# Attention operands laid out by the host: transposes on the chip, a buffer of parts and two early weight conversions taken out of a fused attention, MoE and mixer kernel

## The chip, the cores and the metric

The kernel runs on one core of a Trainium2 chip. The metric is device time in microseconds of one execution, the median of the runs. The engines are TensorE (PE in the profile; its weight loads are PEld), VectorE (DVE), ScalarE (ACT), GpSimd (POOL) and SyncE (SP, which here only issues DMAs). Each engine runs its own instructions strictly in order.

## The reference

Four batches of 576 positions, 8 heads of 64, model width 512. Cut to what is computed:

```python
# attention: q, k, v (4, 8, 576, 64), s (4, 8, 576)
scores = q @ k.T / sqrt(64)
cum = cumsum(maximum(s, 0))                       # along the sequence
scores = where(causal, -1e9, scores + minimum(-(cum_i - cum_j), 0))
attn = softmax(scores);  x = attn @ v             # heads side by side: (4, 576, 512)
# MoE: 8 experts, w1 (8, 512, 1024), w2 (8, 1024, 512); each position goes to one expert e,
# its own argmax or that of the position before, by a gate
x = p[e] * (maximum(x @ w1[e], 0) @ w2[e])
# mixer: U (576, 32), V (32, 576), w_ch1 (512, 2048), w_ch2 (2048, 512)
u = x + (x^T @ U @ V)^T
out = u + maximum(u @ w_ch1, 0) @ w_ch2
```

The inputs come in fp32; w_ch1 and w_ch2 are float64 in memory and come as 8-byte words.

## The kernel before

**Precision by parts.** Each fp32 operand of a large product is split into a high part (a rounded copy, made by ACT, tile type fp32r or f16) and a low part (the operand less its high part, made by DVE or POOL). A product is then high x high + high x low + low x high.

**Stages in time.** Attention with the router runs from 0 to about 290 us, the routing tail (positions scattered to the rows of their experts in DRAM) from there to 323, expert 0 to 367, the other experts to 590, the mixer to the end.

**Attention.** The 32 heads are taken as 16 pairs of neighbouring heads. For a pair n, an operand tile `OP[n % NB]`, with NB = 2, holds four blocks of 576 columns for each head: K1, Q1, K2, Q2, where rows 0 to 63 and 64 to 127 hold different parts, so that one matmul over 128 rows (L706) takes two of the three partial products of the scores and a second over 68 rows (L713) takes the third with the cumulative bias in four more rows. The bias rows come from DRAM (`b_d`, read by `bias(n)` L443). The scores need the head dimension on the partitions, while q and k lie in memory with the position on the rows. So `prep(n)` (L448) does, for each pair:

- loads of two pairs at a time (a group of four heads) into kn, qn, vn, tiles of 128 positions x 5 blocks x 4 heads x 64, in runs of 256 bytes (`load_group` L377, DMAs at L361);
- ten transposes on PE (`blocks`, L468) into PSUM tiles `pt`;
- four ACT copies out of PSUM, the high parts, into a tile `parts` of four blocks, 448 and 128 columns wide (`high`, L475);
- four DVE instructions, the low parts (`low`, L480);
- four DMAs on SP that copy the parts into the operand tile, each head's parts to both halves of the partitions where needed (`stack`, L538, 2 x 576 + 2 x 288 KB). Pair 2 uses free weight tiles (`ring`) in place of `parts`, and twelve DMAs. One `parts` tile exists, so ACT's high parts of the next pair wait until these DMAs have read it (`hold`).

Pair 0 has a path of its own (L1284 to L1325): ACT and DVE copy each head twice side by side, PE transposes the doubled tile, and ACT, DVE and POOL split straight into OP.

The softmax runs in units of one tile of 128 queries and one or two heads: scores on PE into `sp`, the row extremum `nm` on DVE (L730), the exponential on ACT into `Pb` (L747), transposes of it on PE into `pp` (L776), their high part on ACT (`hi`, L784) and low part on DVE (`lo`, L789), the product with V on PE into `ob` (L825), its copy by ACT into `xr` (L837). V is scaled and split on POOL into `VP` (L620 scale, L630 high, L640 low).

**What sets the order.** All of this is recorded as some 1,680 jobs and issued by a table of job numbers, ORDER (L29 to L124), which fixes what stands before what on every engine. The jobs are checked for buffers: `issue` allows a job only when the one that frees its place stands earlier.

**Weights.** Expert weights come in units of 128 columns of w1 (`load_in` L205, DMA L207, 512-byte runs) or 128 rows of w2 (`load_out` L213, DMA L216) into five `raw` buffers, and `conv` (L222) splits a unit into a `ring` tile, high at L226 (POOL) or L230 (ACT), low at L233 (DVE or POOL). Eight units of w1 of expert 0 and, with NEARLY = 2, two units of w2 are converted by POOL beside the attention. The other six units of w2 are converted at the end of the routing tail: four by ACT and DVE, and two by POOL (at 328 to 333 us).

## Time and profile before

| | us |
|---|---|
| three runs | 1011.66, 1013.52, 1017.26 |
| median | 1013.52 |
| the profiled execution itself | 1015.48 |
| its span in the trace | 1013.5 |

| busy in the span | PE | DVE | ACT | POOL |
|---|---|---|---|---|
| us | 936.4 | 567.8 | 453.6 | 361.6 |
| share | 92% | 56% | 45% | 36% |

The page gives one execution. Its shares are means over stages that differ much: DVE and ACT are half busy over the whole, but three quarters busy in the attention and a third or less in the mixer. So the windows by stage are read before any share. A wait is listed with what ended it; an engine that waits costs time only where PE, or whatever stands last in that stage, waits for it in turn. A row of a timeline gives the start, the length, the engine, line, instruction, the tile written and the tile read, and in brackets the idle time just before with its releaser.

### The profile page before, as it was taken

What the parts mean: (1) busy time and instruction counts of PE and PEld (TensorE: products, weight loads), DVE (VectorE), ACT (ScalarE), POOL (GpSimd) and SP (SyncE); (2) the same over time, 40 slices, a digit from 0 to 9 for tenths busy, and PEclk for the clock granted to TensorE, in tenths of its full rate; (3) what the DMA queues carried; (4) which work ended last, traced back from release to release, by engine and by line L of the source; (5) the groups of instructions that cost most, each with busy time, mean ns of one, the idle gap of its engine ahead of it and who ended that gap; (6) DMA issues with size and microseconds to landing.
All of it is one profiled execution on the core that took longest, in us unless ns stands there. A gap on an engine that the chain in (4) does not pass through costs nothing.

```text
span 1013.5 us, 17840 instructions
## 1 busy us (share of the span) xinstructions
PE 936.4 (92%) x6566; PEld 743.1 (73%) x6566; DVE 567.8 (56%) x1124; ACT 453.6 (45%) x1031; POOL 361.6 (36%) x460
## 2 busy tenths in 40 slices
PE   5987989889874999999999979999999999999998
PEld 4777979778763789888888857887666666666676
DVE  6776888776863677677685957882122312211121
ACT  4776878666741466466556753241112102111111
POOL 6632735453744675666767612220000000000000
PEclk9898999898986999999999979999999999999999
DMA  6987999866332876676655332422000200100010
GB/s 177 209 192 163 234 212 227 203 136 159 87 99 68 252 218 185 186 214 212 186 178 166 133 101 65 143 63 82 2 1 1 84 1 1 63 1 0 1 43 21
DMA packets 127423, 120.77 MB, mean 119 GB/s; under 512 B 58407, under 2 KB 99687, under 8 KB 125536
## 3 DMA queue, kind: packets, MB, share of 16 engines
q1 hardware_dynamic: 119264, 105.64, 38.3%
q0 software_dynamic: 6864, 13.63, 4.6%
q8 instruction: 53, 0.87, 0.4%
q10 hardware_dynamic: 1200, 0.30, 0.1%
q14 instruction: 42, 0.34, 0.1%
HBM read 76.84 MB, written 22.30 MB: 98 GB/s over the span
## 4 chain that ended last, share of the span: by engine, by line
PE 63%; DMA 2%; DVE 1%; ACT 1%; issue 1%; SPq 0%; POOL 0%; DVEq 0%; ACTq 0%; POOLq 0%
PE acc L1633 31%; PE ps_h L1621 28%; PE pu L1994 2%; PE ups L2214 1%; DMA raw_in<-in_moe_w_dram 1%; PE xps L1903 1%; DMA raw_out<-in_moe_w_dram 0%; PE ph L2165 0%; DVE c1u L1536 0%; DMA yt_d<-y,idx 0%; DMA ut<-yt_d 0%; ACT y L2062 0%; DVE ul L2217 0%; POOL ring L233 0%; DVE ut L2285 0%
## 5 line engine op out<-in xcount | busy, mean ns | idle before, releaser
L1633 PE MATMUL acc<-ring,hh 128*128 128x512 f32 x928 | 301.6, 406 | 0.0
L1585 DVE SCALAR_TENSOR_TENSOR hl<-ps_h,hh 128x512 fp32r<-128x512 f32 (+6 forms) x144 | 82.3, 572 | 250.6 <-ACT hh L1584 244.1
L1584 ACT ACTIVATE hh<-ps_h 128x512 fp32r<-128x512 f32 (+6 forms) x144 | 72.7, 505 | 330.7 <-PE ps_h L1621 325.2
L1633 PEld LDWEIGHTS acc<-ring,hh 128*128 128x128 f32 x928 | 167.1, 185 | 37.9
L1621 PE MATMUL ps_h<-uh,c1u 128*128 128x256 f16 (+1 forms) x768 | 192.2, 329 | 1.4 <-ACT uh L2216 1.4
L1633 PE MATMUL acc<-ring,hl 128*128 128x512 f32 (+4 forms) x464 | 183.2, 395 | 0.0
L1621 PEld LDWEIGHTS <-c1u 128*128 128x128 f16 x1152 | 108.0, 99 | 85.9 <-issue 21.9
L1621 PE MATMUL ps_h<-ul,c1u 128*128 128x256 f16 (+1 forms) x384 | 125.9, 328 | 0.9 <-DVE ul L2217 0.9
L1621 PE MATMUL ps_h<-xh,ring 128*128 128x384 f32 (+5 forms) x512 | 123.8, 314 | 2.1 <-DVE hl L1585 2.0
L233 POOL TENSOR_TENSOR ring<-raw_out,ring 128x512 fp32r<-128x512 f32 x60 | 80.2, 1339 | 69.0 <-ACT ring L230 67.5
L1633 PEld LDWEIGHTS acc<-ring,hl 128*128 128x128 f32 (+4 forms) x464 | 85.7, 185 | 22.2 <-DVE hl L1585 0.3
L789 DVE SCALAR_TENSOR_TENSOR lo<-pp,hi 128x384 f16<-128x384 f32 (+2 forms) x160 | 85.4, 550 | 22.1 <-ACT hi L784 20.6
L2206 POOL TENSOR_SCALAR us<-ut,up 128x512 f32<-128x512 f32 x9 | 6.7, 739 | 252.9 <-DVE up L2190 252.9
L1621 PEld LDWEIGHTS ps_h<-xh,ring 128*128 128x128 f32 x512 | 88.4, 188 | 6.4 <-DVE hl L1585 3.4
L784 ACT ACTIVATE hi<-pp 128x384 f16<-128x384 f32 (+2 forms) x160 | 77.2, 496 | 27.2 <-PE pp L776 20.5
L776 PE MATMUL pp<-ident,Pb 128*128 128x128 f32 x480 | 83.8, 297 | 4.7 <-DVE lo L789 2.6
L747 ACT ACTIVATE Pb<-sp,nm 128x192 f32<-128x192 f32 (+4 forms) x160 | 80.9, 537 | 6.8 <-DVE nm L730 5.7
L233 DVE TENSOR_TENSOR ring<-raw_in,ring 128x512 fp32r<-128x512 f32 x56 | 59.1, 1056 | 37.8 <-ACT ring L230 37.6
L1621 PE MATMUL ps_h<-xl,ring 128*128 128x384 f32 (+5 forms) x256 | 79.8, 312 | 0.2 <-DVE xl L1909 0.2
L706 PE MATMUL sp<-OP 128*128 128x288 f32 (+4 forms) x192 | 71.8, 379 | 7.9 <-DMA OP<-parts 3.2
L730 DVE TENSOR_REDUCE nm<-sp 128x1 f32<-128x576 f32 (+4 forms) x96 | 67.6, 704 | 14.7 <-PE sp L721 12.7
L713 PE MATMUL sp<-OP 68*128 68x288 f32 (+4 forms) x192 | 61.4, 324 | 2.2 <-DMA OP<-b_d 2.2
(249 smaller groups left out, 1579.5 us busy)
## 6 DMA issues: line engine op xcount, KB each, us to landing
raw_in<-in_moe_w_dram SPq DMA_DIRECT2D x64, 256.0 KB
raw_out<-in_moe_w_dram SPq DMA_DIRECT2D x64, 256.0 KB
raw<-in_moe_w_ch_dram SPq DMA_DIRECT2D x32, 512.0 KB
OP<-parts SPq DMA_DIRECT2D x28, 576.0 KB
OP<-parts SPq DMA_DIRECT2D x28, 288.0 KB
kn<-in_k_dram SPq DMA_DIRECT2D x32, 128.0 KB
x_d<-x SPq DMA_DIRECT2D x16, 256.0 KB
out_dram<-ut SPq DMA_DIRECT2D x4, 1024.0 KB
```

The costliest lines, as they stand in the source:

```text
L233: lo_eng.tensor_tensor(out=lo, in0=src, in1=hi.bitcast(F32), op=ALU.subtract)
L706: nc.tensor.matmul(sp[:, c, :cw], lhsT=W1[j][:, h, t * P : (t + 1) * P], rhs=K1[j][:, h, c0 : c0 + cw], start=True, stop=False,)
L713: nc.tensor.matmul(sp[:, c, :cw], lhsT=W2[j][0:SK, h, t * P : (t + 1) * P], rhs=K2[j][0:SK, h, c0 : c0 + cw], start=False, stop=not diag,)
L730: nc.vector.tensor_reduce(out=k["nm"] if two else k["nm"][:, 0:1], in_=k["sp"], op=ALU.min, axis=AX.X if two else AX.XY,)
L747: nc.scalar.activation(out_, in_, AF.Exp, scale=-1.0, bias=k["nm"][:, x : x + 1])
L776: nc.tensor.transpose(pp[:, i - i0], k["pb"][:, a, x * P : (x + 1) * P], ident)
L784: nc.scalar.activation(k["hi"][:, i0:i1], k["pp", i0][:, : i1 - i0], AF.Copy, scale=SCALE)
L789: nc.vector.scalar_tensor_tensor(out=k["lo"][:, i0:i1], in0=k["pp", i0][:, : i1 - i0], scalar=SCALE, in1=k["hi"][:, i0:i1], op0=ALU.mult, ...
L1584: nc.scalar.activation(hh[:, :n], ps[:, :n], AF.Relu)
L1585: nc.vector.scalar_tensor_tensor(out=hl[:, :n], in0=ps[:, :n], scalar=0.0, in1=hh[:, :n].bitcast(F32), op0=ALU.max, op1=ALU.subtract,)
L1621: nc.tensor.matmul(ps[f][:, x * cut : (x + 1) * cut], lhsT=wa[:, kk], rhs=xa[:, kk, :cut], start=(kk == 0 and i == 0), stop=(kk == KD - 1 ...
L1633: nc.tensor.matmul(acc[i][0:m], lhsT=ha[:, sl], rhs=u2[g][:, wa], start=(g == 0 and jj == 0), stop=(g == nf - 1 and jj == 2),)
```

## The change

**Layout by the host.** q and k come transposed per pair (`qT`, `kT`: pair, 128 rows of two heads x 64, 576 columns), v comes per group as one block of 128 x 1280 (`vG`), and w1 and w_ch1 come in blocks of 128 columns, so that a unit is one run of 2 KB (w1) or 4 KB (w_ch1) per partition.

**Pairs.** kn and qn become two tiles each of 128 x 2 heads x 576. A pair's load puts both heads into rows 0 to 63 and again into rows 64 to 127: four DMAs of 288 KB per pair in runs of 2304 bytes. From these tiles the parts go straight into OP, of which there are now three (NB = 3). There is no `parts` tile, no transposes of q and k on PE, no `hold`, and no path of its own for pair 0, except that DVE instead of POOL makes its low key half.

```diff
-    NEARLY = 2
+    NEARLY = 0
...
-        NB = 2
+        NB = 3
...
+        def load_turned(src, dst, n, eng):
+            for r in range(2):
                 eng.dma_start(
+                    dst[n % NG][r * D : (r + 1) * D], src[n].rearrange("(h d) s -> d h s", d=D)
+                )
...
+        def split_steps(n, eng):
+            j = n % NB
+            kd, qd = kn[n % NG], qn[n % NG]
+            kh_, qh_, kl_, qh2 = K1[j], Q1[j], K2[j][0:D], Q2[j][0:D]
+            sc = -(D**-0.5)
+
+            def key_high():
+                nc.scalar.copy(kh_, kd)
+
+            def key_low():
+                eng.tensor_tensor(
+                    out=kl_, in0=kd[0:D], in1=kh_[0:D].bitcast(F32), op=ALU.subtract
+                )
+
+            def query_high():
+                nc.scalar.activation(qh_, qd, AF.Copy, scale=sc)
+
+            def query_again():
+                nc.sync.dma_start(qh2.bitcast(F32), qh_[0:D].bitcast(F32))
+
+            def query_low():
                 nc.vector.scalar_tensor_tensor(
+                    out=qh_[D:P],
+                    in0=qd[D:P],
+                    scalar=sc,
+                    in1=qh_[D:P].bitcast(F32),
                     op0=ALU.mult,
                     op1=ALU.subtract,
                 )
...
+            kh_, kl_, qh_, q2_, ql_ = split_steps(n, nc.gpsimd)
+            a = job("A", 1070, kh_, [loaded[0]] + old)
+            b_ = job("P", 2800, kl_, [a])
+            c = job("A", 1070, qh_, [loaded[1]] + old)
+            d = job("SP", 900, q2_, [c])
+            e_ = job("D", 1800, ql_, [c])
+            f = job("SP", 675, lambda: bias(n), old)
...
+            old = stacks.get(n - NG, [])
+            k_load[n] = job("SP", 800, lambda: load_turned(kT, kn, n, nc.sync), old[0:2])
+            q_load[n] = job("SP", 800, lambda: load_turned(qT, qn, n, nc.sync), old[2:5])
...
-            w1[ds(e, 1), :, f * P : (f + 1) * P].rearrange("o (k p) c -> p (o k) c", p=P),
+            w1[ds(e, 1), f].rearrange("o p (k c) -> p (o k) c", k=KD),
```

A load of pair n waits for the steps that read the same tile for pair n - 2. ORDER is replaced by a table for the new jobs. **Weights.** With NEARLY = 0 no unit of w2 is converted beside the attention; at the end of the routing tail ACT and DVE convert four as before, and POOL four instead of two.

What the new order does to the queues shows at three places. **SP at the start**, from the bias rows of pair 0 on; `kn`, `qn` are the loaded keys and queries, `OP` the operand tiles. Before:

```order
L443 DMA OP_132<-b_d 4x2x1152
L367 DMA kn_114<-in_k_dram 64x2x64
L371 DMA kn_114<-in_k_dram 128x4x64 x2
L367 DMA qn_116<-in_q_dram 64x2x64
L371 DMA qn_116<-in_q_dram 128x4x64 x2
L361 DMA qn_117<-in_q_dram 64x4x64
L361 DMA qn_117<-in_q_dram 128x4x64 x4
```

And after the change:

```order
L427 DMA OP_126<-b_d 4x2x1152
L358 DMA kn_113<-in_kT_dram 64x2x576 x2
L358 DMA qn_115<-in_qT_dram 64x2x576 x2
L452 DMA OP_126<-OP_126 64x2x576
L358 DMA kn_112<-in_kT_dram 64x2x576 x2
L358 DMA qn_114<-in_qT_dram 64x2x576 x2
L427 DMA OP_127<-b_d 4x2x1152
L427 DMA OP_128<-b_d 4x2x1152
```

The copy of the high query half of pair 0 (L452), without which that pair has no scores, stands behind the bias rows and the four loads of pair 1.

**POOL at the first V** (`vn` the loaded V, `vsc` its scale, `VP` its parts). Before:

```order
L361 DMA vn_119<-in_v_dram 64x4x64
L361 DMA vn_119<-in_v_dram 128x4x64 x4
L620 TENSOR_SCALAR vn_118<-vn_118,vsc 128x5x128
L630 TENSOR_SCALAR VP_156<-vn_118 128x10x64
L620 TENSOR_SCALAR vn_118<-vn_118,vsc 128x5x128
```

And after the change:

```order
L363 DMA vn_117<-in_vG_dram 128x1280
L444 TENSOR_TENSOR OP_127<-kn_113,OP_127 64x2x576
L444 TENSOR_TENSOR OP_128<-kn_112,OP_128 64x2x576
L548 TENSOR_SCALAR vn_116<-vn_116,vsc 128x5x128
L558 TENSOR_SCALAR VP_147<-vn_116 128x10x64
```

The low key halves of pairs 1 and 2 (L444) stand ahead of the scaling and splitting of the first V.

**DVE in the middle of a pair**, at the preparation of pair 5 beside the softmax of an earlier one (`nm` the row extremum, `lo` the low part of the exponentials). Before:

```order
L480 SCALAR_TENSOR_TENSOR parts<-pt,parts 128x128 x2
L730 TENSOR_REDUCE nm<-sp 128x1
L480 SCALAR_TENSOR_TENSOR parts<-pt,parts 128x448 x2
L730 TENSOR_REDUCE nm<-sp 128x2
L789 SCALAR_TENSOR_TENSOR lo<-pp,hi 128x384 x2
```

And after the change:

```order
L658 TENSOR_REDUCE nm<-sp 128x1
L455 SCALAR_TENSOR_TENSOR OP_128<-qn_115,OP_128 64x2x576
L658 TENSOR_REDUCE nm<-sp 128x2
L717 SCALAR_TENSOR_TENSOR lo<-pp,hi 128x384 x2
L545 COPY vsc<-ob 128x2
```

Four instructions that read one tile in PSUM and one in SBUF have become one of 1152 columns with both inputs in SBUF; reductions and low parts stand behind it as they did behind the four.

## Rows read from the trace of the kernel before

**Rows 1.** Page, part 1: busy time and share; part 2: the granted PE clock.

```profile
PE 936.4 (92%) x6566; PEld 743.1 (73%) x6566; DVE 567.8 (56%) x1124; ACT 453.6 (45%) x1031; POOL 361.6 (36%) x460
PEclk9898999898986999999999979999999999999999
```

**Rows 2.** Windows: length, then PE, PEld, DVE, ACT, POOL busy, PEclk, DMA, GB/s.

```profile
12.00:30.00 18.00, 14.64 (x78) 12.27 (x78) 11.46 (x30) 10.05 (x26) 11.68 (x22) 0.87 0.89 214
30.00:290.00 260.00, 231.53 (x2824) 206.24 (x2822) 194.41 (x468) 188.48 (x496) 131.73 (x195) 0.94 0.75 176
160.00:180.00 20.00, 19.97 (x256) 17.95 (x252) 16.24 (x43) 16.39 (x43) 13.54 (x18) 1.00 0.89 214
323.00:367.00 44.00, 40.90 (x208) 35.63 (x206) 27.33 (x41) 21.65 (x45) 25.43 (x27) 1.00 0.72 215
612.00:1013.50 401.50, 396.22 (x2063) 273.98 (x2062) 135.50 (x237) 79.73 (x156) 23.56 (x21) 1.00 0.11 36
```

**Rows 3.** Timeline: PE at the first scores, ACT at the last exponential.

```profile
12.50 0.59 PE L706 MATMUL sp<-OP 128*128 128x288 f32 x1
...
285.82 0.74 ACT L747 ACTIVATE Pb<-sp,nm 128x576 f32<-128x576 f32 x1
```

**Rows 4.** Waits, 12 to 300 us: total us, times, longest.

```profile
POOL tail L936 <- DVE t L289: 18.4, 1, 18.4
PE pt L468 <- DVE parts L480: 3.2, 2, 1.6
PE sp L706 <- DMA OP<-parts: 3.2, 2, 2.4
PE pp L776 <- DVE parts L480: 1.4, 2, 0.8
```

**Rows 5.** Groups by form, 0 to 290 us: busy us, mean ns | idle before.

```profile
L480 DVE SCALAR_TENSOR_TENSOR parts<-pt,parts 128x448 fp32r<-128x448 f32 x28 | 17.0, 618 | 7.1 <-ACT parts L475 7.0
L475 ACT ACTIVATE parts<-pt 128x448 fp32r<-128x448 f32 x28 | 14.9, 553 | 11.5 <-DMA OP<-parts 7.5 <-PE pt L468 3.3 <-issue 0.4
L468 PE MATMUL pt<-ident,kn 128*128 128x128 f32 x75 | 14.7, 301 | 4.5 <-DVE parts L480 3.2 <-DVE lo L789 1.3
L468 PE MATMUL pt<-ident,qn 128*128 128x128 f32 x75 | 13.4, 284 | 0.0
L577 ACT ACTIVATE vabs<-vn 128x640 bf16<-128x640 f32 x16 | 11.8, 739 | 0.0
...
L480 DVE SCALAR_TENSOR_TENSOR parts<-pt,parts 128x128 fp32r<-128x128 f32 x28 | 6.7, 282 | 7.7 <-ACT parts L475 7.7
L475 ACT ACTIVATE parts<-pt 128x128 fp32r<-128x128 f32 x28 | 6.3, 283 | 9.7 <-issue 4.5 <-PE pt L468 3.2 <-DMA OP<-parts 1.9
```

**Rows 6.** Timeline of PE: four transposes in quick succession.

```profile
18.82 0.60 PE L468 MATMUL pt<-ident,qn 128*128 128x128 f32 x4
```

**Rows 7.** Timelines of expert 0: a DVE subtraction alone, and beside POOL.

```profile
333.71 0.68 DVE L233 TENSOR_TENSOR ring<-raw_in,ring 128x512 fp32r<-128x512 f32 x1
...
345.30 3.64 DVE L233 TENSOR_TENSOR ring<-raw_in,ring 128x512 fp32r<-128x512 f32 x1
...
345.83 2.54 POOL L233 TENSOR_TENSOR ring<-raw_out,ring 128x512 fp32r<-128x512 f32 x2
```

**Rows 8.** Timelines of ACT and SP at the start; SPq is the issuing of a DMA.

```profile
4.85 0.72 ACT L1323 COPY kn<-kn 128x640 f32<-128x640 f32 x1 [0.42 <-DMA kn<-in_k_dram]
...
9.85 0.30 SPq L443 DMA_DIRECT2D OP<-b_d  x1
13.87 2.92 SPq L361 DMA_DIRECT2D qn<-in_q_dram  x5
```

**Rows 9.** Timeline of POOL and chain that ended last, expert 0.

```profile
328.83 0.62 POOL L226 TENSOR_SCALAR ring<-raw_out 128x512 fp32r<-128x512 f32 x1 [10.39 <-DMA raw_out<-in_moe_w_dram]
...
330.96 8.45 DMA raw_in<-in_moe_w_dram
```

**Rows 10.** Window 160 to 180, L747 alone: ACT busy (count), PEclk, DMA, GB/s.

```profile
160.00:180.00 20.00, 6.44 (x13) 1.00 0.89 214
```

More of the change, by code (lines that the diff above doesn't have):

```diff
@@ L130 @@
     tc: tile.TileContext,
[L131 to L133 removed]
+    qT: bass.AP,
+    kT: bass.AP,
+    vG: bass.AP,
     s: bass.AP,
@@ L509, in prep @@
-            box = {}
-            def turn():
-                box["p"] = ps_t.tile([P, 512], F32, tag="t", name="pt")
-                for x, (_, src, _, _) in enumerate(sides):
-                    blocks(src, 4, 5, box["p"], x)
-            def both(f):
-                for x, (name, _, scale, _) in enumerate(sides):
-                    f(box["p"][:, x * P : (x + 1) * P], name, W4, P, scale)
-            a = job("PE", 218, turn, list(loaded), ("t",))
-            b_ = job("A", 314, lambda: both(high), [a] + hold)
@@ L1332 @@
+        load_turned(kT, kn, 1, nc.sync)
+        load_turned(qT, qn, 1, nc.sync)
+        nc.gpsimd.dma_start(vn[0].rearrange("p t h d -> p (t h d)"), vG[0])
+        for step in split_steps(0, nc.vector):
+            step()
         for x in P_all:
@@ L1361 @@
             if n >= 1:
-                if n % 2 == 0 and g not in k_load:
-                    group_jobs(g)
-                old = [s_of[u] for u, x in enumerate(units) if x[0] == n - 2 and u in s_of]
-                hold = [] if n < 3 else stacks[n - 1][1:] if n > 3 else stacks[1][1:]
-                stacks[n], turned[n] = prep(n, old, hold, (k_load[g], q_load[g]))
+                if n >= NG:
+                    load_jobs(n)
+                old = [s_of[u] for u, x in enumerate(units) if x[0] == n - NB and u in s_of]
+                loaded = [x for x in (k_load.get(n), q_load.get(n))]
+                stacks[n] = prep(n, old, loaded)
             if n % 2 == 0 and g not in v_load:
@@ L2326 @@
     arrays, args = {}, []
-    for name in _INS:
-        a = _np.ascontiguousarray(inputs[name])
+    for name, a in _laid_out(**inputs).items():
+        a = _np.ascontiguousarray(a)
         if a.dtype == _np.float64:
```

227 lines of the change are left out of this document (49 added, 178 removed), and 183 rows, old and new, of the table ORDER.

## The prediction, blind

> **What bounds the kernel now.** I read the totals of the page first, then the windows by stage, then inside the attention stage the waits, the groups of instructions and the moment at which its first and last work stands. The totals say TensorE: 936.4 of 1013.5 us busy [rows 1]. The windows say where that is not the whole story. In the mixer (612 to 1013.5) PE is busy 396.22 of 401.5 us and in expert 0 40.90 of 44 [rows 2], so a transfer or a conversion that gets cheaper there is worth the remainder at most, 5 and 3 us. The stage with room is the attention, 12 to 290: PE idles 18.00 - 14.64 + 260.00 - 231.53 = 31.8 us, DVE is busy 205.9, ACT 198.5 and POOL 143.4 of 278 us. PE is nearest its limit, but three more engines hand tiles to each other there, so a step taken off PE is worth its time only where the others keep up. The pace: first scores at 12.50, last exponential at 285.82 [rows 3], so 16 head pairs in 273.3 us, 17.1 us each. The DMA share in 12:30 and 160:180 is 0.89, yet in the second of these PE is busy 19.97 of 20 us [rows 2]: the transfers are dense but PE does not wait for them in that stretch.
>
> **The change, part by part.** Quoted sums go against the profiled execution, 1015.48 us; it stands 1.96 us above the median of 1013.52.
>
> *PE loses the transposes of q and k.* Ten per pair on 15 pairs: 14.7 + 13.4 = 28.1 us of busy time, 1.87 us a pair [rows 5]. Busy times of neighbours overlap: four in quick succession take 0.60 us together [rows 6], and with one lasting 284 ns a further one costs (0.60 - 0.28) / 3 = 0.105 us, so ten cost at least 1.05 us. Between 16 and 28 us for 15 pairs; I take 1.4 us a pair, a little under the middle, because PE runs at the higher of its two clock levels (2.4 GHz) for most of the stage (PEclk 0.94 over 30:290 [rows 2]): **-21**.
>
> *The chain behind them goes.* PE waited 3.2 us for the parts to leave PSUM before the next transposes, 3.2 us for the copies of the parts and 1.4 us for the same DVE step ahead of the transposes of P [rows 4], 7.8 us in all. In their place the scores of a pair now wait for one 288 KB copy of the high query half and for two low halves. These are due one to two pairs ahead since there are three operand tiles instead of two. Between 0 and 7.8 comes back; I take half: **-4**.
>
> *ACT gets longer instructions.* Before: 14.9 + 6.3 us in 14 pairs, 1.5 us a pair [rows 5]. After: two copies of 128x1152 from SBUF. The nearest row is the 128x640 one at 739 ns; from 128 to 448 columns the rows rise by 270 ns, 0.84 ns a column, so 739 + 512 x 0.84 = 1.17, about 1.2 us each, 2.4 us a pair: +0.9 us, +13 us over 15 pairs, and ACT stands at 212 us of a stage then some 255 us long (83%). PE's idle time that the parts did not cause is 31.8 - 7.8 = 24 us, under a tenth of the stage; between none and all of the 13 us reaches PE, and I charge 2: **+2**.
>
> *DVE trades four PSUM reads for one SBUF instruction.* Before 17.0 + 6.7 us in 14 pairs, 1.7 us a pair. After: one 64x1152 instruction with both inputs in SBUF. The nearest row is the subtraction of 128x512 at 0.68 us when nothing else is there [rows 7], 1.33 ns a column, so 1.5 us: nothing gained or lost, if undisturbed. The same line took 3.64 us when POOL ran its own subtraction beside it, 2.96 us more [rows 7]. I take 1.5 to 2 us and **0**, and keep the 2.96 for the rival.
>
> The Trainium skill, "SBUF — State Buffer", section "Who interferes with whom", speaks against this part: a VectorE instruction with two SBUF inputs contends with a GpSimd instruction that reads SBUF, and whichever comes second blocks for the whole instruction. The pair of rows above agrees with it (3.64 against 0.68). Before, the low halves had one input in PSUM; after, both engines carry such an instruction for each pair. If every one collided, the sum would be that of the second rival instead of this term's 0.
>
> *POOL takes the low key half.* At 2.54 us for two of 128x512 [rows 7] one of 1152 columns is 2.9 us, 43 us for 15 pairs; the two second-weight conversions that leave are 2 x (0.62 + 1.27) = 3.8 us [rows 7, 9]. POOL goes from 143 to about 182 us of 255. In its queue the first two key halves now stand ahead of the scaling of the first V; what waits behind them is the V of pair 0, then P x V of pair 0 on PE, which is work that is stretched out there anyway. POOL also stood 18.4 us in the router constants waiting for DVE [rows 4]; the key half of pair 5 stands behind that, two pairs ahead of its use. Cost 0, up to 3 us at the start, which is in the next term.
>
> *The start.* Before, the heads came singly: ACT could begin at 4.85 with the first keys, and first scores ran at 12.50 [rows 3, 8]. After, 1.18 MB (each head in both halves) must land instead of 0.59 MB. The high query half is then copied by a DMA that stands on SP behind the bias read, which was issued at 9.85, and behind four loads of pair 1. An issue of that kind takes 2.92 / 5 = 0.58 us [rows 8], so it is issued at 9.85 + 0.3 + 4 x 0.6 = 12.6. It lands some 2.5 us later if nothing is in its way, 5.5 us later if the 1.18 MB of pair 1 go first at 214 GB/s [rows 2]: first scores at 15 to 18, both heads together. **+4**, from 2.5 to 6.
>
> *Expert 0.* Two more units of the second weights are loaded and converted on POOL beside it (+3.8 us of POOL, with POOL already waiting 10.39 us for such loads), while the longest transfer on the chain there, 8.45 us [rows 9], comes in pieces of 2 KB instead of 512 B. PE idles only 3.1 us there, so -3 is the best; the worst I put at +3, two loads of 256 KB more in the way. I take **-1**. The later experts and the mixer: 0, hidden by PE's own work.
>
> Sum: -21 - 4 + 2 + 0 + 4 - 1 = -20; 1015.5 - 20 = 995.5 in a profile, 993.5 as a median, **994 us**.
>
> **Rivals.** (1) *The freed PE time is given back.* ACT, which sits 198.5 of 278 us, gets 13 us more, and if all of it reaches PE together with waits for the new copies, the sum is -16 + 13 + 4 - 1 = 0, so 1009 to 1018. For it: in 30:290 PE already waits with ACT at 72%. Against: 160:180, where PE is busy 19.97 of 20 us with ACT at 16.39 and DVE at 16.24 [rows 2], so the others can keep up with a PE that never stops.
>
> (2) *Slower: the low halves block each other.* Place: the DVE instruction on the query low half against POOL's reads. Price: 2.96 us a time [rows 7], on 15 pairs 44 us of DVE, 206 + 42 = 248 us of a stage of 255; DVE then becomes the bound, since the reductions that release the exponentials and the low parts of P stand behind it in its queue. Each us of delay a pair that reaches PE costs 15 us, so it eats the gain of 20 at 1.3 us a pair and is past 5 us slower at 1.7. At 2 us a pair: 993.5 + 30 = 1024; at the full 2.96, 1037. For it: POOL would be reading SBUF most of the time (about 70% busy). Against: an instruction of POOL has on average only part of its length left when DVE arrives, and DVE has 72 us of slack before.
>
> (3) *More is gained.* In 160:180 there were 13 exponentials in 20 us [rows 10], at 10 a pair 15.4 us a pair against the mean of 17.1. If the simpler chain lets the whole stage run at that pace less 1.05 us, 16 x 2.7 = 44 us; with the start, -40: 973. For it: PE's waits for the parts vanish. Against: the router's work and the causal shapes fall unevenly, and PEclk is 0.94 over the stage, not the 1.00 of that window.
>
> (4) *It does not do what it says*: the copy of the high query half and the loads, which wait for the tile of two pairs before, stand in one SP queue, so one late step would hold the next pair's loads. That gives a few us of PE waiting per pair early on and none later, -20 + 10: 1004. It lies inside the range.
>
> **How the numbers follow.** The forecast with its own bounds (980 to 1003): 0.58. Rival 3: 0.08. Rival 4: 0.12, faster still. Rival 1: 0.10. Rival 2: 0.12. A measurement of this kernel tells some 0.5% from no change, so faster means below 1008.5 and slower above 1018.6: 0.78 faster, 0.10 the same, 0.12 slower. The range must leave out 0.2: rival 2 above and half of rival 3 below, so 975 to 1013.
>
> **What would show it.** In the changed profile: PE has no instruction that writes pt and its busy time falls by about 28 us and by what pair 0's own transposes take; first scores at 15 to 18; the last exponential near 268 instead of 285.82; ACT's 128x1152 copies near 1.2 us; DVE's 64x1152 instruction at 1.5 us in most pairs; POOL's near 2.9; the stretch from the last exponential to the end unchanged within 3 us. The forecast is wrong if PE's idle time in the stage grows by more than 10 us (rival 1), if DVE's instruction averages over 3 us and P's low parts or the row maxima wait for it (rival 2), or if the late stages move by more than 5 us, which no row here explains.

## The result, and the profile after

The change makes the kernel a little slower: 1016.74 us against 1010.7 (medians of 20 runs each, taken together on one chip). The ratio is 1.009, with a 95% interval of 1.007 to 1.011: 7 to 11 us. It compares fast runs alone, those within 1.5% of the fastest of their kernel, and so it can differ from the ratio of the medians, here 1.006. The prediction, 994 (975 to 1013), said 20 us faster.

The profiled execution took 1015.21 us with a span of 1013.5, the span of the one of before. That is chance: the profiled run of before stands 4.8 us above its 20-run median, that of after 1.5 below. So the two traces are compared stage by stage. The page's totals and clock of after (answering to [rows 1]):

```profile
PE 924.0 (91%) x6396; PEld 730.7 (72%) x6396; DVE 569.5 (56%) x1071; ACT 462.1 (46%) x993; POOL 390.6 (39%) x448
...
PEclk9999998897985999999999979999999999999999
```

The 170 transposes are gone from PE, but its busy time fell by 12.4 us, where 28 was forecast. The windows of [rows 2] in the trace of after (length, then busy time and count of PE, PEld, DVE, ACT, POOL; PEclk, DMA share, GB/s):

```profile
12.00:30.00 18.00, 6.98 (x25) 5.11 (x25) 3.29 (x5) 3.69 (x7) 0.58 (x2) 1.00 0.80 190
30.00:290.00 260.00, 227.94 (x2671) 200.33 (x2670) 200.29 (x437) 200.72 (x476) 167.25 (x200) 0.94 0.49 125
160.00:180.00 20.00, 16.29 (x158) 14.89 (x158) 12.83 (x32) 12.48 (x30) 10.70 (x12) 0.80 0.61 155
323.00:367.00 44.00, 41.98 (x214) 37.32 (x213) 29.81 (x42) 23.12 (x46) 30.85 (x31) 0.97 0.72 228
612.00:1013.50 401.50, 396.55 (x2063) 274.09 (x2062) 135.23 (x237) 79.74 (x156) 23.58 (x21) 1.00 0.11 36
```

The first 18 us hold 25 matmuls where there were 78. From 12 to 290 us PE now idles 43.1 us, where it idled 31.8: it has less to do, and the stage is no shorter for it. The mixer has not moved. The stretch 160 to 180, where PE never stopped before, now has a granted clock of 0.80 and 3.7 us of idle PE.

The 1.00 in the first row is no sign of a fast PE. By the lengths of one and the same score matmul PE ran at the lower of its two clock levels (1.2 GHz) up to about 52 us: 0.44 us at 24.55 and still at 49.39, as in 139.50 to 141.00, where the granted clock reads 0.50, against 0.30 at 141.97. In the trace of before a score matmul of this width takes 0.29 us already at 37.45.

```profile
24.55 0.44 PE L641 MATMUL sp<-OP 68*128 68x288 f32 x1
...
49.39 0.44 PE L641 MATMUL sp<-OP 68*128 68x288 f32 x1
...
140.43 0.44 PE L641 MATMUL sp<-OP 68*128 68x288 f32 x1
...
141.97 0.30 PE L641 MATMUL sp<-OP 68*128 68x288 f32 x1
```

Progress through the pairs, read as the time of the first score matmul of a pair in PE's timeline (us), shows where the time goes; these columns are worked out from some hundred such rows and are used for the experiments too ("pairs 5 to 13" is the time from the start of pair 5 to that of pair 13, eight pairs). Four of the rows of before, and four of after:

```profile
37.24 0.38 PE L706 MATMUL sp<-OP 128*128 128x288 f32 x1
...
104.22 0.38 PE L706 MATMUL sp<-OP 128*128 128x288 f32 x1
...
235.07 0.38 PE L706 MATMUL sp<-OP 128*128 128x288 f32 x1
...
280.59 0.38 PE L706 MATMUL sp<-OP 128*128 128x288 f32 x1
```

```profile
47.80 0.59 PE L634 MATMUL sp<-OP 128*128 128x288 f32 x1
...
108.91 0.38 PE L634 MATMUL sp<-OP 128*128 128x288 f32 x1
...
244.22 0.40 PE L634 MATMUL sp<-OP 128*128 128x288 f32 x1 [0.90 <-ACT Pb L675]
...
285.74 0.38 PE L634 MATMUL sp<-OP 128*128 128x288 f32 x1
```

| | pair 1 | pair 5 | pairs 5 to 13 | pair 15 | end of span |
|---|---|---|---|---|---|
| before | 37.2 | 104.2 | 130.9 | 280.6 | 1013.5 |
| after | 47.8 | 108.9 | 135.3 | 285.7 | 1013.5 |

The start costs 10.6 us, of which pairs 1 to 4 win back 5.9 (they had the most to wait for before). Pairs 5 to 13 in steady pace should have won 1.4 us of PE time a pair, 11 in all; they lost 4.4. Pairs 13 and 14 win 4.0 (41.5 against 45.5). From pair 1 to pair 15 the change is thus the faster by 5.5 us, 237.9 against 243.4.

Each of these numbers carries the scatter of single traces. Kernels with the attention of before (e3 and e4 below; e4 with two weight conversions fewer on POOL) take 131.7 and 136.4 us in pairs 5 to 13 and 246.3 and 248.8 from pair 1 to pair 15; kernels with the attention of after, but for pair 0 (e1 and e5), 137.5 and 137.1, and 239.8 and 240.2. On the mean of three each the change loses some 4 us in pairs 5 to 13 and wins some 7 from pair 1 to pair 15, of 25 that were forecast. From pair 15 to the end the trace of before takes 732.9 us and that of after 727.8; these 5 us can't be told from scatter, since two kernels with the same code there, e5 and e12, differ by 8 (727.8 and 735.7).

**The start.** Timelines of SP, ACT, PE and POOL of after (start, length, engine, line, instruction; in brackets the idle time before it and what ended it), answering to [rows 3, 8]:

```profile
8.89 1.15 ACT L441 CAST OP<-kn 128x1152 fp32r<-128x1152 f32 x1 [5.10 <-DMA kn<-in_kT_dram]
11.64 0.30 SPq L427 DMA_DIRECT2D OP<-b_d  x1
...
13.28 1.25 SPq L358 DMA_DIRECT2D qn<-in_qT_dram  x2
14.58 0.62 SPq L452 DMA_DIRECT2D OP<-OP  x1
...
23.21 0.58 PE L641 MATMUL sp<-OP 68*128 68x288 f32 x1 [9.73 <-DMA OP<-OP]
...
30.12 5.20 POOL L444 TENSOR_TENSOR OP<-kn,OP 64x1152 fp32r<-64x1152 f32 x2 [17.55 <-ACT OP L441]
35.32 0.80 POOL L548 TENSOR_SCALAR vn<-vn,vsc 128x640 f32<-128x640 f32 x1
```

The keys land 4 us later than the first head did; the copy of the high query half is issued at 14.58 and is there at 23.21, 8.6 us later; and V of pair 0 is scaled only behind two key halves on POOL, at 35.32.

**The steady pairs.** The new steps by group (busy us, mean ns, idle before with what ended it), then the DVE instruction's shortest, median and longest, then it in the middle of the attention and what PE does next:

```profile
L444 POOL TENSOR_TENSOR OP<-kn,OP 64x1152 fp32r<-64x1152 f32 x15 | 41.1, 2745 | 57.3 <-ACT OP L441 57.3
L455 DVE SCALAR_TENSOR_TENSOR OP<-qn,OP 64x1152 fp32r<-64x1152 f32 x16 | 25.9, 1619 | 0.5
L449 ACT ACTIVATE OP<-qn 128x1152 fp32r<-128x1152 f32 x16 | 18.6, 1164 | 0.0
L441 ACT CAST OP<-kn 128x1152 fp32r<-128x1152 f32 x16 | 18.4, 1159 | 5.1 <-DMA kn<-in_kT_dram 5.1
```

```profile
L455 DVE SCALAR_TENSOR_TENSOR OP<-qn,OP x16: 1354/1355/2727, 11.5 to 258.6; 64x1152 fp32r<-64x1152 f32 x16
```

```profile
170.83 2.73 DVE L455 SCALAR_TENSOR_TENSOR OP<-qn,OP 64x1152 fp32r<-64x1152 f32 x1
...
175.23 0.55 PE L540 MATMUL ob<-vbit,ones 1*128 1x2 f32 x2 [1.81 <-DVE lg L948]
```

And the window behind that wait, in the columns of [rows 2]:

```profile
175.30:182.00 6.70, 6.70 (x32) 6.45 (x33) 2.60 (x6) 5.57 (x11) 4.38 (x3) 0.50 0.47 123
```

The lengths of ACT, DVE undisturbed and POOL are those forecast (1.2, 1.5 and 2.9 us). But DVE's instruction runs to 2.73 us at times, PE waits 1.81 us for what stands behind it on DVE, and the next 6.7 us run at a granted clock of 0.50. The same pattern stands at 136.8 and 194.8 us. Not each such wait goes with it: in the trace of before one of 1.64 us ends at 200.89, and the granted clock behind it, to 207 us, is 1.00. In pairs 5 to 13 the two traces read:

```profile
104.20:235.10 130.90, 118.72 (x1447) 105.61 (x1445) 102.01 (x249) 97.29 (x255) 67.94 (x85) 0.95 0.86 203
```

```profile
108.90:244.20 135.30, 116.43 (x1366) 102.18 (x1364) 104.01 (x227) 102.98 (x242) 85.47 (x89) 0.91 0.54 143
```

PE has 81 matmuls fewer and is busy only 2.3 us less. Its clock was short of full speed by 0.09 of 135.3 us, 12.2 us, against 0.05 of 130.9, 6.5 us; and it idles 18.9 us against 12.2. The idle time is the part that other traces bear out: 19.6 and 18.9 us in e1 and e5, 9.0 and 7.9 in e3 and e4. The clock is not: e1 and e5 read 0.90, but e3 and e4, with the attention of before, 0.91 and 0.86. At the same 0.91 the trace of e3 reads:

```profile
107.50:239.20 131.70, 122.66 (x1446) 109.89 (x1444) 102.52 (x249) 97.19 (x255) 66.57 (x83) 0.91 0.84 198
```

So at an equal clock 80 matmuls fewer take 6.2 us off PE in these eight pairs, some 0.8 us a pair, and PE waits 9.8 us longer.

### The profile page after: what moved, and what is told of

Same layout as the page of the kernel before. It is cut to its first block, busy times and chain, and to the rows that moved or that the text cites. A ratio compares the mean times of both kernels' runs of the same rounds, so it can differ in the third digit from the quotient of the medians.

```text
span 1013.5 us, 17227 instructions
## 1 busy us (share of the span) xinstructions
PE 924.0 (91%) x6396; PEld 730.7 (72%) x6396; DVE 569.5 (56%) x1071; ACT 462.1 (46%) x993; POOL 390.6 (39%) x448
## 3 DMA queue, kind: packets, MB, share of 16 engines
q1 hardware_dynamic: 46608, 93.21, 31.8%
## 4 chain that ended last, share of the span: by engine, by line
PE 64%; DMA 1%; DVE 1%; issue 1%; ACT 1%; SPq 0%; DVEq 0%; ACTq 0%
PE acc L1509 31%; PE ps_h L1497 29%; PE pu L1868 2%; PE ups L2088 1%; PE xps L1777 1%; DMA raw_in<-in_w_dram 0%; PE ph L2039 0%; DVE c1u L1412 0%; DMA ut<-yt_d 0%; DMA yt_d<-y,idx 0%; ACT y L1936 0%; DVE ul L2091 0%; SPq L212 0%; DVE ut L2159 0%; ACT uh L2090 0%
## 5 line engine op out<-in xcount | busy, mean ns | idle before, releaser
L1497 PE MATMUL ps_h<-xh,ring 128*128 128x384 f32 (+5 forms) x512 | 124.1, 314 | 2.0 <-DVE hl L1461 2.0
L675 ACT ACTIVATE Pb<-sp,nm 128x192 f32<-128x192 f32 (+4 forms) x160 | 80.6, 539 | 31.8 <-DVE nm L658 28.5
L634 PE MATMUL sp<-OP 128*128 128x288 f32 (+4 forms) x192 | 74.0, 390 | 18.2 <-DVE OP L455 12.9
```

The source lines that it names most:

```text
L634: nc.tensor.matmul(sp[:, c, :cw], lhsT=W1[j][:, h, t * P : (t + 1) * P], rhs=K1[j][:, h, c0 : c0 + cw], start=True, stop=False,)
L675: nc.scalar.activation(out_, in_, AF.Exp, scale=-1.0, bias=k["nm"][:, x : x + 1])
L1497: nc.tensor.matmul(ps[f][:, x * cut : (x + 1) * cut], lhsT=wa[:, kk], rhs=xa[:, kk, :cut], start=(kk == 0 and i == 0), stop=(kk == KD - 1 ...
```

## The experiments

Each kernel was timed beside the kernel before on the same chip; ratios are to it, with 95% intervals. Where the expectations call theories by letters, the text behind each says in words what stands and what falls. Kernels of different chips are compared by their ratios. The first question was which of four things takes the gain: the start, the weights, a PE whose time is worth nothing, or the other engines.

**e1: the first copy ahead of the loads of pair 1** (edit of the changed kernel):

```diff
         bias(0)
-        load_turned(kT, kn, 1, nc.sync)
-        load_turned(qT, qn, 1, nc.sync)
...
             step()
+        load_turned(kT, kn, 1, nc.sync)
+        load_turned(qT, qn, 1, nc.sync)
```

> The changed kernel with one move at the start: pair 0's steps, with the copy of its high query half, stand on SP ahead of the four loads of pair 1. Theory A (the start costs the time): in the changed kernel the copy landed at 23.2 us because 1.18 MB of pair 1 went first, and the delay of some 10 us against the kernel before (first scores at 12.50) is carried to the end. Then first scores run through at 14 to 16 us and the time falls by 7 to 9 us against the changed kernel, to a ratio of 0.998 to 1.003 with the kernel before. Rival B (something later sets the pace, so that a later start is made up for): the last exponential stays within 3 us of 289.8 and the ratio stays at 1.006 to 1.011.

Measured: 1013.32, ratio 1.006 [1.002, 1.009]; pair 1 at 43.7. The copy was issued 2.6 us sooner but still took 7.4 us:

```profile
19.42 0.58 PE L641 MATMUL sp<-OP 68*128 68x288 f32 x1 [5.83 <-DMA OP<-OP]
```

By the middle of the intervals the start is part of the loss, though they overlap. The place on SP is only part of the start: later in the trace of after such a copy lands 3.2 us after its issue at best and 5.1 in the median, so what is issued beside and behind this one probably holds it up. No run separates that.

**e2: PE is given time back** (edit of the changed kernel; ten matmuls a pair whose result is overwritten):

```diff
+                    if cw >= P:
+                        nc.tensor.matmul(
+                            sp[:, c, :P],
+                            lhsT=W1[j][:, h, t * P : (t + 1) * P],
+                            rhs=K1[j][:, h, c0 : c0 + P],
...
```

> The changed kernel with ten matmuls of 128 columns a pair more on PE, whose results are overwritten: PE has about as much to do as with the ten transposes that the change took out. Theory C (after the start PE's freed time turns into short waits and into stretches at the lower clock level, so it is worth little): within 4 us of the changed kernel, ratio 1.005 to 1.013 with the kernel before, and PEclk in 109 to 244 us above the 0.91 of the changed kernel. Rival D (PE is still the bound in the attention, and the freed time was a gain that something else ate): 10 x 0.105 us x 16 = 17 us slower than the changed kernel, ratio 1.022 to 1.028.

Measured: six runs from 1018.7 to 1035.5, ratio 1.0125 [1.003, 1.022]; the page of the profiled one:

```profile
PE 938.3 (92%) x6556; PEld 745.8 (73%) x6556; DVE 572.8 (56%) x1071; ACT 462.5 (45%) x993; POOL 391.4 (38%) x448
```

14.3 us of PE cost 9.9 us of span in the profiled runs (1023.4 against 1013.5), and 8.1 of these stand there by pair 15 (293.8 against 285.7). By this pair of traces PE's time has a price of some 0.7 us a us, and the 12.4 us that the change took off it should have been worth 9. The timed runs scatter too widely to confirm it: against the change's own 1.009 they allow anything from a gain of 6 us to a loss of 13, the middle in C's range and the end in D's. C's other sign did not come: pairs 5 to 13 read a granted clock of 0.91, not above it. So e2 does not decide between C and D; these traces speak against a PE whose time is worth nothing.

**e3 and e4: the weights** (edits of the kernel before: w1 and w_ch1 laid out by the host, and NEARLY = 0):

```diff
-            w1[ds(e, 1), :, f * P : (f + 1) * P].rearrange("o (k p) c -> p (o k) c", p=P),
+            w1[ds(e, 1), f].rearrange("o p (k c) -> p (o k) c", k=KD),
...
-    NEARLY = 2
+    NEARLY = 0
```

> The kernel before with only w1 and w_ch1 laid out by the host, so that their loads come in runs of 2 and 4 KB; q, k and v as before. Theory: the weights do not bear on the time, since PE waits 3 us in expert 0 and hardly later: ratio 0.996 to 1.002. Rival: denser loads beside the attention and in expert 0 take something off: 3 to 6 us, ratio 0.994 to 0.997. The other rival, that they cost time by getting in the way of other transfers, gives 1.003 to 1.006.

> The kernel before with no second weights converted beside the attention (NEARLY = 0), all else as before: POOL converts four units instead of two beside expert 0. Theory: POOL is 3.8 us longer busy at expert 0 where it waits 10 us anyway, and 3.8 us freer in the attention where it is not the bound: ratio 0.998 to 1.003. Rival: the two later units delay the positions of expert 1 on POOL and the weights of expert 0: 3 to 5 us slower, 1.003 to 1.005, with PE idle over 6 us in 323 to 367.

Measured: 1009.99, ratio 1.002 [0.998, 1.006], and 1011.75, ratio 0.997 [0.991, 1.002]. No effect that can be told, so the loss is not in the weights, as far as each of the two edits alone can show it. That leaves the attention.

**e5: pair 0's copy made by POOL** (edit of the changed kernel):

```diff
             def query_again():
+                if n == 0:
+                    nc.gpsimd.tensor_copy(qh2, qh_[0:D].bitcast(F32))
+                    return
```

> The changed kernel with the copy of pair 0's high query half made by POOL, as in the kernel before, instead of a DMA. Putting the DMA first (e1) brought the first scores through at 19.4 instead of 23.2 us and took about 3.4 us off the median. Theory A (each us at the start is carried to the end): first scores through at 14 to 15 us, 8 to 9 us less than the changed kernel, ratio 0.999 to 1.003 with the kernel before. Rival B (the pace of the later pairs takes it back): the fifth pair starts at most 4 us before the changed kernel's and the ratio stays at 1.005 or more.

Measured: 1012.88, ratio 1.006 [1.003, 1.009]. The scores go through at 14.34, 9 us sooner, and yet pair 1 stands at 42.4, 5 us sooner and still 5 us later than before. ACT's timeline shows what is in the way: it stands 3.62 us for the keys of pair 2, with exponentials behind them, and PE then waits 3.92 us for these.

```profile
24.79 1.15 ACT L441 CAST OP<-kn 128x1152 fp32r<-128x1152 f32 x1 [3.62 <-DMA kn<-in_kT_dram]
...
26.84 0.42 PE L637 MATMUL sp<-OP 128*128 128x64 f32 x1 [3.92 <-ACT Pb L678]
```

From 25 to 43 us PE then runs at a granted clock of 0.50. By the ratios (1.009 against 1.006) both ways of mending the start bring some 3 us, with intervals that overlap the change's own. But they mend only 4.1 and 5.4 of its 10.6 us; what the rest costs they don't show.

**e6, e7, e8: one engine relieved at a time**, from pair 3 on (edits of the changed kernel; one is shown, the others cut ACT's two copies to 640 columns and POOL's key half to 128 in the same way; the parts of the other columns are left out, while PE's instructions stay as many, 6396):

```diff
             def query_low():
+                c_ = S if n < 3 else 64
                 nc.vector.scalar_tensor_tensor(
-                    out=qh_[D:P],
-                    in0=qd[D:P],
+                    out=qh_[D:P, :, 0:c_],
+                    in0=qd[D:P, :, 0:c_],
```

> The changed kernel with the two ACT copies of pairs 3 to 15 made 640 columns wide instead of 1152 (320 of each head; the high parts of the other columns are left out), so that ACT spends 1.5 us a pair on them, as the kernel before did. Theory E (ACT's longer instructions stand ahead of the high parts of P, the exponentials and the copies out of ob, and are what takes PE's gain): 8 to 13 us less than the changed kernel, ratio 0.996 to 1.001. If ACT is not the cause: within 3 us of the changed kernel, ratio 1.006 to 1.012.

> The changed kernel with POOL's low key part of pairs 3 to 15 made 128 columns wide instead of 1152 (the rest of the low key parts is left out): POOL loses some 2.4 us a pair, and with it most of what it can collide with on DVE. Theory F (the low key half on POOL delays V and blocks DVE): 8 us or more less than the changed kernel, ratio below 1.001, and DVE's low query part falls from 1.62 us to 1.35 us. Without F: within 3 us of the changed kernel, ratio 1.006 to 1.012.

> The changed kernel with DVE's low query part of pairs 3 to 15 made 128 columns wide instead of 1152 (the rest of the low query parts is left out): DVE loses some 1.4 us a pair and no long instruction stands ahead of the row extrema and the low parts of P. Theory G (one long DVE instruction in the place of four short ones takes the gain): 8 us or more less than the changed kernel, ratio below 1.001. Without G: 2 to 5 us less, since some work is gone, ratio 1.003 to 1.008.

Measured: ACT 1017.74, ratio 1.009 [1.006, 1.012]; POOL 1019.38, 1.010 [1.007, 1.014]; DVE **1001.64, 0.9935 [0.990, 0.997]**. Of the three only DVE's relief brings anything: 14.5 us less of it brings 15. That more comes back through the clock than through the waits is seen in its pairs 5 to 13, to be held against those of after:

```profile
106.90:232.30 125.40, 109.40 (x1365) 94.96 (x1363) 96.32 (x227) 101.87 (x242) 81.83 (x88) 0.97 0.59 154
```

The same matmuls take 7.0 us less of busy time, at 0.97 in place of 0.91, and PE idles 2.9 us less. (e14 below reads 0.97 again; e1, e5, e6 and e7, with DVE's step unchanged, 0.87 to 0.90.) POOL's relief took most of the key half away as DVE's neighbour, and brought nothing. The ACT run tells less than it should: DVE's instruction, unchanged, met POOL at other moments and averaged 2.1 us instead of 1.6, and one such meeting (see e14) put pair 1 off to 51.5:

```profile
L457 DVE SCALAR_TENSOR_TENSOR OP<-qn,OP 64x1152 fp32r<-64x1152 f32 x16 | 33.7, 2108 | 0.5
```

**e9: the DVE instruction in four pieces**, up to two other DVE instructions between them (edit of the changed kernel):

```diff
-            e_ = job("D", 1800, ql_, [c])
+            e_ = job("D", 450, lambda: ql_(0, 1, 0, S // 2), [c])
+            for a0, c0 in ((0, S // 2), (1, 0), (1, S // 2)):
...
```

> The changed kernel with DVE's low query part of each pair after the first made in four instructions of 64x288, with up to two other DVE instructions between them, instead of one of 64x1152. The run that narrowed it (e8) fell by 15 us, against 18 us of DVE time taken away. Theory H (it is the length of one instruction ahead of row extrema and low parts of P that costs): the pieces let these through, 5 to 12 us less than the changed kernel, ratio 0.996 to 1.003. Theory I (it is DVE's time as such, which PE's chain contains): no better than the changed kernel, and 0 to 6 us more for four starts instead of one, ratio 1.006 to 1.014.

Measured: 1052.0, ratio 1.040 [1.037, 1.044]. Were it only the length of one instruction that keeps the others waiting, this should have helped. Instead DVE's time itself grew:

```profile
L455 DVE SCALAR_TENSOR_TENSOR OP<-qn,OP 64x288 fp32r<-64x288 f32 x60 | 44.8, 763 | 1.4
```

A piece takes 449 ns at its shortest, 456 in the median, 763 in the mean and 2758 at most: each piece can be held up by itself, for about as long as a whole one. DVE's 20.3 us more (44.8 and 1.4 for pair 0, against 25.9) became some 32 us (1.040 against 1.009), so that no help from the shorter pieces is left over.

**e10 and e15: the same load put on the kernel before** (a 64x1152 subtraction on DVE, or an ACT copy of 832 columns, in each pair, of no use):

```diff
+                nc.vector.tensor_tensor(
+                    out=junk,
+                    in0=kn[i][0:D].rearrange("p t h d -> p (t h d)")[:, 0 : 2 * S],
...
+                nc.scalar.copy(junk, kn[i].rearrange("p t h d -> p (t h d)")[:, 0:832])
```

> The kernel before with one more DVE instruction a pair (a subtraction of 64x1152 from SBUF into an unused tile) behind the four low parts, about 1.5 us: the price of DVE time in the kernel before. Theory I (DVE's time lies on the chain in both kernels): 10 to 18 us slower than the kernel before, ratio 1.010 to 1.018. Otherwise (DVE had 72 us of slack in the attention before, and only the change made it count): within 4 us, ratio 0.996 to 1.004.

> The kernel before with one more ACT copy a pair (128x832 into an unused tile, about 0.9 us), on 15 pairs 13.5 us: what the change adds to ACT, and nothing else. Theory J: 6 to 12 us slower than the kernel before, ratio 1.006 to 1.012, about the price that one more DVE instruction had in e10 (21.2 us of DVE for 8 to 10 us). If ACT's time lies beside the chain, as the prediction had it: within 3 us, ratio 0.997 to 1.003.

Measured: 21.2 us of DVE cost 1021.13, ratio 1.010 [1.006, 1.013], half a us a us; 13.5 us of ACT cost 1017.07, 1.003 [1.001, 1.004], some 3 us or a fifth: near the 2 that the prediction charged for ACT's 13 us. DVE's time was no free reserve in the kernel before either.

**e11 and e12: DVE's or POOL's work moved** (edits of e5: the query low half on POOL from pair 1 on, with ACT scaling in place first; the key low halves of pairs 1 and 2 on DVE):

```diff
+                    nc.scalar.activation(qd, qd, AF.Copy, scale=sc)
+                    nc.scalar.copy(qh_, qd)
...
-            kh_, kl_, qh_, q2_, ql_ = split_steps(n, nc.gpsimd)
+            kh_, kl_, qh_, q2_, ql_ = split_steps(n, nc.vector if n < 3 else nc.gpsimd)
```

> The changed kernel with pair 0's copy on POOL, and for all later pairs the low query part on POOL: ACT scales the query tile in place first (one more copy of 128x1152 a pair), then POOL subtracts. DVE loses 1.6 us a pair, ACT gains 1.2 and POOL 2.7. With DVE's time on the chain and ACT and POOL off it (e6 and e7 showed no gain from relieving them): 12 to 18 us less than the changed kernel, ratio 0.988 to 0.996. If ACT or POOL then becomes the bound (POOL at some 208 of 260 us, ACT at 218): no gain or a loss against e5, ratio 1.003 or more.

> The changed kernel with pair 0's copy on POOL and the low key parts of pairs 1 and 2 on DVE, so that POOL scales the first V without waiting for them. In e5 pair 1 started at 42.4 us against 37.2 in the kernel before, with POOL's two key parts ahead of the first V until 31.5. Theory A: pair 1 starts at 37 to 39 us, 3 to 5 us less than e5, ratio 1.000 to 1.003. Rival: DVE's 2.7 us more at that place cost what POOL's way saves: same as e5, 1.004 to 1.008.

Measured: 1032.32, ratio 1.019 [1.015, 1.023], where DVE's waits for ACT's `hi` from 48 to 300 us are 42.5 us, against 28.7 after the change; and 1023.7, 1.012 [1.008, 1.016], with V scaled at 24.0 instead of 28.6 but pair 1 no sooner (43.1), since ACT stands for the keys of pair 2 as in e5 (4.07 us), and, in the profiled run, 4 us more than e5 by pair 15 and 8 more behind it, which these runs don't explain. POOL with ACT's help cannot take DVE's step for nothing; e12 says little.

**e14: DVE and ACT relieved together** (e8, with ACT's copies cut to 640 columns; the rest is left out as there):

```diff
+            w_ = S if n < 3 else 320
...
-                nc.scalar.copy(kh_, kd)
+                nc.scalar.copy(kh_[:, :, 0:w_], kd[:, :, 0:w_])
```

> e8 (DVE's low query part of pairs 3 to 15 narrowed to 128 columns) with the two ACT copies of these pairs made 640 columns wide as well (work left out in both). Against e8, with DVE's instruction too short to be blocked for long, this is ACT's price alone: ACT loses 0.85 x 13 = 11 us. Theory J (ACT's longer copies take a good part of PE's gain): 6 to 10 us less than e8, ratio 0.984 to 0.988. If ACT's time lies beside the chain: within 2 us of e8, ratio 0.992 to 0.996.

Measured: 1012.39, ratio 0.999 [0.997, 1.001]. Pairs 5 to 13 take 124.1 us, against 125.4 with DVE alone relieved: ACT's time adds nothing in the steady pairs. That it is slower than e8 as a whole (0.999 against 0.9935) comes from the start (pair 1 at 51.5) and from behind pair 15. At the start DVE's still whole instruction of pair 2 took 5.25 us, beside two of POOL, and PE waited 3.77 us for what stands behind it:

```profile
44.03 5.25 DVE L458 SCALAR_TENSOR_TENSOR OP<-qn,OP 64x1152 fp32r<-64x1152 f32 x1
...
44.09 2.65 POOL L446 TENSOR_TENSOR OP<-kn,OP 64x1152 fp32r<-64x1152 f32 x1
46.67 1.38 POOL L571 TENSOR_TENSOR VP<-vn,VP 128x640 f16<-128x640 f32 x1
```

In the trace of after POOL's key half begins 0.36 us behind DVE's instruction there, not 0.06; DVE takes 1.36 us and POOL 3.47. So the same two steps cost PE almost 4 us or nothing by a third of a us. From pair 15 to the end of expert 0 e14 takes 8.5 us more than e8, at a granted clock of 0.80 against 0.87; why it is lower stays open.

**e13: each head split once, on all 128 partitions** (edit of the changed kernel). A pair is loaded once, as 128x576; ACT, POOL and DVE split it in place at half the columns, and eight copies on SP bring the parts to OP; pair 0 is as in e5:

```diff
+            def query_low():
+                nc.vector.scalar_tensor_tensor(
+                    out=qd[:, 1].bitcast(F32R),
+                    in0=qd[:, 1],
+                    scalar=sc,
+                    in1=qd[:, 0],
...
+            def query_moves():
+                for h in range(2):
+                    x = qd[h * D : (h + 1) * D]
+                    nc.sync.dma_start(blocks(h, 0, 1), x[:, 0:1].to_broadcast([D, 2, S]))
+                    nc.sync.dma_start(Q1[j][D:P, h].bitcast(F32), x[:, 1])
```

> A whole version built on the account so far: pair 0 with its copy on POOL as in e5; for the later pairs each head is loaded once (128x576), ACT, POOL and DVE split 128x576 tiles in place (0.7, 1.4 and 0.8 us instead of 1.16, 2.75 and 1.62 us an instruction), and eight DMAs a pair put the parts into the operand tile, as the kernel before did, but without transposes. Per pair ACT loses 0.9 us, DVE 0.8, POOL 1.3 against e5; DMA gains 0.9 MB. If engine time on ACT and DVE is what takes the gain: 15 us or more less than e5, ratio 0.985 to 0.995 with the kernel before. If not, or if the copies now hold up the scores: ratio 1.000 or more, with PE waiting for these copies.

Measured: 1009.88, ratio 0.998 [0.995, 1.001]. Pairs 1 to 8 went by at 13.4 us each, then ACT's timeline shows one long stop:

```profile
158.11 0.74 ACT L554 ACTIVATE vabs<-vn 128x640 bf16<-128x640 f32 x1 [10.87 <-DMA vn<-in_vG_dram]
```

The load of that V stood on SP behind a copy that waited 7.8 us, until DVE's low half was done.

**e16: e13 with every V load issued by POOL. e17: e16 with the query side as in the change** (loaded twice, ACT 128x1152, DVE 64x1152, one copy):

```diff
-            (nc.gpsimd if g <= 3 else nc.sync).dma_start(
+            nc.gpsimd.dma_start(
...
-            if n > 0:
+            if n > 0 and src is kT:
                 eng.dma_start(dst[n % NG][:, 1], src[n])
...
-            d = job("SP", 0, lambda: None, [c])
+            d = job("SP", 900, q2_, [c])
```

> e13 with all loads of V issued from POOL instead of SP, so that they stand behind no copy. If the stall at pair 8 was that load: ACT waits for V under 2 us there, the pairs up to 12 run at 13 to 15 us each, and the time falls by 9 to 14 us against e13, ratio 0.984 to 0.990 with the kernel before: a version faster than both. If the stall comes back in another place (SP's copies wait for DVE and hold the key loads or the bias rows): within 4 us of e13, ratio 0.994 to 1.000.

> e16 with the query side as in the changed kernel: loaded twice, one ACT copy of 128x1152, one DVE instruction of 64x1152, one DMA; only the keys are split once, by 128x576 instructions of ACT and POOL. If DVE's long instruction is the greater part of what takes PE's gain: 6 to 12 us slower than e16, ratio 0.993 to 1.000. If it is the key side, or ACT and POOL time, that counts: within 3 us of e16.

Measured: e16 **1000.2, ratio 0.986 [0.983, 0.989]**, which beats both kernels; e17 1017.34, ratio 1.003 [1.0005, 1.005]. The query side as the change has it costs 17 us: DVE's instruction, but with it ACT's longer copy and the second load of the queries. DVE's group in e16 and in e17:

```profile
L495 DVE SCALAR_TENSOR_TENSOR qn<-qn 128x576 fp32r<-128x576 f32 x15 | 13.5, 902 | 0.0
```

```profile
L461 DVE SCALAR_TENSOR_TENSOR OP<-qn,OP 64x1152 fp32r<-64x1152 f32 x16 | 26.6, 1663 | 0.5
```

And the window from 104 to 244 us of e16 and of e17:

```profile
104.00:244.00 140.00, 127.92 (x1567) 112.02 (x1566) 110.66 (x258) 106.63 (x272) 85.91 (x107) 0.95 0.79 212
```

```profile
104.00:244.00 140.00, 123.59 (x1338) 108.82 (x1337) 105.19 (x230) 96.62 (x236) 78.03 (x90) 0.84 0.63 167
```

With 11 us less of DVE for the stage, PE does 229 matmuls more in the same 140 us, at 0.95 instead of 0.84. The key side, loaded and split once in both, doesn't bring it. (In e16's trace pair 15 begins 22.7 us sooner than after the change and the span is 12.7 us shorter; by the ratios, 0.986 against 1.009, e16 is 23 us faster. What of the 10 us behind pair 15 is one trace's scatter, these runs don't say.)

## Why the prediction failed, step by step

- **PE, "-21", and the chain, "-4": counted whole, it came in part.** These 25 us were to come through because the others keep up. From pair 1 to pair 15 the traces show 5.5 us, on the mean of three each some 7. Part is size: PE's busy time fell by 12.4 us in all, where 28 was forecast, and at an equal clock by some 0.8 us a pair, where 1.4 was taken. The rest was given back to waits: in pairs 5 to 13 PE idles 18.9 us against 12.2 (9.0 and 7.9 in e3 and e4). The step also took the clock of before as given; but from 0.86 to 0.95 in traces with the attention of before, it is no fixed number there either.
- **DVE, "0": why the others did not keep up, and the step that failed.** "Nothing gained or lost" was true of the undisturbed instruction (1.355 us; 1.5 was forecast) and of the busy time (569.5 us against 567.8 in all). But the price of DVE's time was put at nothing, on a sum that left 72 us of slack. The runs show that a us of DVE in this place costs half a us before the change (e10) and about one after it (e8; 1.6 in e9), because maxima, low parts and scales stand behind it in order and PE waits for them. Rival 2 named the place and the mechanism, with a price that was too high: 6 of the 16 instructions were held up, by 4.2 us in all, not by 2.96 each. The Trainium skill, "SBUF — State Buffer", section "Who interferes with whom", says that such a DVE instruction and a POOL instruction that reads SBUF block each other whole; the trace agrees in kind (1.354 alone, up to 2.73).
- **The waits.** Those of [rows 4] on the parts went, and others came, as the waits of after from 12 to 300 us show (total us, times, longest). The 12.9 and the 9.7 are the start, the former counted from 0; the others are those of the pairs:

```profile
DVE lo L717 <- ACT hi L712: 33.1, 39, 2.6
PE sp L634 <- DVE OP L455: 12.9, 1, 12.9
PE sp L641 <- DMA OP<-OP: 9.7, 1, 9.7
PE sp L634 <- ACT Pb L675: 5.2, 8, 0.9
PE pp L704 <- DVE lo L717: 4.4, 6, 1.4
```

- **The start, "+4": too small.** The scores go through at 23.2, not at 15 to 18: the bias rows are issued at 11.64 where 9.85 was taken over from before, and the copy took 8.6 us where 2.5 to 5.5 were allowed. At pair 1 this is 10.6 us. Mended by 4.1 and 5.4 us it brought some 3 each time (e1, e5); that this comes near the +4 is luck, since neither mends the whole.
- **ACT, "+2"; POOL, 0; expert 0 and the weights, -1.** Right within what can be told: e15 and e14, e7, e3 and e4. ACT's copies measure 1.16 us.
- **Rival 1** had the right sum, by luck, with the wrong engine: the greater part of the gain was given back, but not to ACT (e14, e15). Its sign was met: PE's idle time in the stage grew by 11.3 us, though 7.7 of these lie before 30 us. Rival 3's argument, that 160:180 shows the pace the others can keep, fell with that window, which after the change has PE idle for 3.7 us.

The sum with what was measured: +10.6 for the start and -5 to -7 for the pairs makes +4 to +5, where the 20 runs say +6 (medians) to +9 (ratio); behind pair 15 the traces can't be told apart. **What stays open:** whether the one DVE instruction costs more than the four that it replaced, for no run took the low halves off the kernel before, and e8 and e17 show only what DVE's step is worth in the changed kernel. Also how much of its price is its being held up by POOL and how much its mere length in that place (e7 took most of POOL's key half away, yet DVE's instruction still averaged 1.54 us and nothing was gained), and how much of e17's 17 us is ACT's query copy and the second load.

## What to carry to other kernels

An engine that is half busy is no reserve where it works in order and PE waits for the instructions behind the new one: price its time by the queue, not by its share. Spread such an instruction over all partitions rather than half of them (0.90 us in place of 1.66 in the mean for as many values), and let DMAs copy the parts. Don't weigh stages of a few us on one trace each: nearly like code differed here by 4.7 us in eight pairs (e3, e4). And where one queue issues both loads and copies that wait for an engine, the loads behind them wait as well; another engine's queue sets them free (e16).

## What the hardware showed beyond what was expected

- Four DVE pieces of 64x288 with both inputs in SBUF took 763 ns in the mean where 449 is the shortest, up to 2758 (e9): a hold-up strikes a piece like a whole instruction, so cutting up multiplied it here. A whole one of 64x1152, 1.355 us alone, took 5.25 us when two POOL instructions that read SBUF began 0.06 and 2.64 us behind it (e14).
- A copy of 288 KB issued ahead of the next pair's loads still landed 7.4 us later (e1), where the one behind them took 8.6.
- PE waits of 1.4 to 1.9 us, with PE busy on either side, were followed by stretches at a granted clock of 0.50, 6.7 us long after the wait that ends at 175.23; not all were (1.64 us at 200.89 before). With less DVE work in front, the mean clock of the same pairs was 0.97 in place of 0.91 (e8).
- DVE's instruction of 128x576 took 0.90 us in the mean, that of 64x1152 on the same number of values 1.66 (e16, e17).
